# Gate work of part 1 in blocks of four pieces in every other step

## The chip, the cores and the metric

The kernel runs on one core of a Trainium2 chip. Times are device microseconds (us) of one execution. PE is TensorE (matmuls; PEld its weight loads), DVE VectorE, ACT ScalarE, POOL GpSimd, SP the engine that issues most DMAs. L12 is line 12 of the kernel.

## The reference

A gated recurrence over 4 batches of 8 heads, 768 positions and 48 values, and then a multiplicative feed-forward on its output, all float32:

```python
for t in range(S):
    state = alpha[:, :, t, :, None] * state + einsum('bhd,bhe->bhde', k[:, :, t], v[:, :, t])
    y[:, :, t] = einsum('bhd,bhde->bhe', q[:, :, t], state)
x = y.transpose(0, 2, 1, 3).reshape(3072, 384)
out = (((x @ w1) * (x @ w2)) @ w3) @ w_out      # w1, w2: 384 x 1024, w3: 1024 x 1024, w_out: 1024 x 384
```

## The kernel before

The recurrence is computed in 24 chunks of 128 positions, six to a batch. Part 1 is a loop over 25 steps (n = 0 to 24, L726); step n works on several chunks at once, as a pipeline. The feed-forward starts inside it: as soon as three or four chunks of x are there, the products x @ w1 and x @ w2 of these chunks (the "gates") are spread over the steps. The rest of the feed-forward follows after the loop (L824 on) on PE, with the weights w3 and w_out folded into one.

Float32 products that must be exact are made of three parts, high, low and mixed, each in a form that PE takes at its faster rate. So each factor of a gate is 3 x 3 = 9 matmuls (`products`, L554), and `exact` (L557) puts them together: parts 0 and 1 into one PSUM bank, copied by ACT (L563), part 2 into another, added by DVE (L565). [...]

**Pieces.** A piece is one factor of one gate: nine matmuls, one L563, one L565. Two pieces make a gate; the second one ends with the product of both factors on DVE (L602), and then the store of the gate before it is issued on SP (`store_ab`, L628). Gates wait in the queue `fill`, and `run(k)` (L691) takes k pieces from it. Four gates (eight pieces) come into it in steps 9, 13 and 17, eight gates (512 columns wide instead of 384) in step 21; before that `split_early` (L527; L521 on ACT, L522 and L524 on DVE) has split x.

**One step n from 10 on**, in the written order, with what it puts on the engines:

- loads for later steps on SP: alpha of n+5 (L145), k and q of n+4 (L151, L152), v of n+2 (L157), stores of x (L305);
- `attend_state(n-1)` (L474), which needs the state from `outer` and `advance`;
- `scores(n)` (L430), interleaved with `attend_low(n-1)` (L419); then the masks on DVE, four instructions of L440, which empty the two banks of the scores. `attend_low(n)` and `attend(n)` of the next step read the masked scores `ms`;
- `transposed(n+1)` (L381), copied to `qkT` by ACT (L383, two instructions); the scores of n+1 need it;
- in steps 9, 13, 17, 21 `split_early`;
- `attend(n-1)` (L482), copied by ACT (L489); `outer(n)` (L393, not in the last chunk of a batch: 5, 11, 17, 23), added by DVE (L403);
- the first piece, `run(pieces > 0)`;
- `decayed(n+2)` on DVE (L359) and `logs(n+4)` (L324, L328 on ACT, L329 on DVE);
- the second piece, `run(pieces > 1)`;
- `decays(n+3)` (L346), with two exponentials on ACT (L349, L350);
- one or two quarters of a weight conversion (`convert`: L245, L248, L251 to L253, L262, L265 on DVE; L244, L249, L260 on ACT);
- the third piece, `run(pieces > 2)`.

The order of each engine's queue is fixed before the kernel runs, by a planner that starts from the written order and may put an instruction ahead that it expects to be ready earlier. On PE the pieces stand in the trace where the code has them; on DVE, ACT and SP later work is often drawn forward. On the chip each engine works through its queue in that order.

The number of pieces in steps 10 to 24 is 3, 3, 2, 0, again and again: eight pieces in four steps.

Of the kernel before, what the change touches and what calls it, by code (L numbers as in the profile page):

```python
# [48 lines left out]
def kernel(  # L49
# [86 lines left out]
    def load_a(n):  # L136
        if paired(n):
            if n % 2 == 0:
                b, c = divmod(n, NCH)
                x = pairs[n // 2 % 2]  # L140
                nc.sync.dma_start(out=x.rearrange("p h s d -> p h (s d)"), in_=alpha[b, :, ds(c * C, 2 * C), :].rearrange("h (p s) d -> p h (s d)", s=2))
                st["a", n] = st["a", n + 1] = x
        elif n < N:
            st["a", n] = inp.tile([C, H, D], FP32, tag="ac", name="ac", bufs=2)
            nc.sync.dma_start(out=st["a", n], in_=rows(alpha, n))  # L145

    def load_kq(n):
        if n >= N:
            return
        st["kq", n] = inp.tile([C, 2, H, D], FP32, tag="kq", name="kq")  # L150
        nc.sync.dma_start(out=st["kq", n][:, 0], in_=rows(k, n))  # L151
        nc.sync.dma_start(out=st["kq", n][:, 1], in_=rows(q, n))  # L152

    def load_v(n):
        if n < N:
            st["v", n] = vs[n % len(vs)]
            (nc.gpsimd if 2 < n < 8 else nc.sync).dma_start(out=st["v", n][:, :, 0:D], in_=rows(v, n))  # L157
# [122 lines left out]
    def fetch(ahead=3):  # L280
        while weights and len(begun) < ahead:
            begun.append(weights.popleft())
            next(begun[-1])
# [17 lines left out]
    def store():  # L301

        while later:
            dst, src = later.popleft()
            nc.sync.dma_start(out=dst, in_=src)  # L305
# [109 lines left out]
    def attend_low(n, jj, i, half):  # L415

        s, w = ds(DP * i, DP), (vts[n % 2] if i else st["v", n])
        h = half * NP // 2 + jj
        nc.tensor.matmul(st["y", n][0][i][ds(DP * half, DP), jj, 0:DP], w[s, h if i else 2 * h, :],  # L419
                         st["ms", n][s, i, h, 0:DP], start=(n % NCH == 0 and jj == 0), stop=True, skip_group_check=True)  # L420
# [25 lines left out]
    def scores(n):  # L446
        if turned(n):
            return turned_scores(n)
        qkT = st["qkT", n]
        sc = [bank().rearrange("p (j c) -> p j c", j=NP) for _ in range(2)]  # L450
        for j in range(NP):
            for i in range(2):
                r = ds(DP * i, D)
                nc.tensor.matmul(sc[i][:, j, :], qkT[r, 0, j, :], qkT[r, 1, j, :], start=True, stop=True)  # L454
        ms = work.tile([C, 2, NP, C], FP32, tag="ms", name="ms")
        for i in range(2):
            masked = nc.vector.tensor_tensor(ms[:, i].bitcast(I32), sc[i].bitcast(I32), keep_bc, op=ALU.bitwise_and)
        ends_of_part1[0] = mark["ms", n] = masked.ins
        st["ms", n] = ms
# [3 lines left out]
    def attend_state(n):  # L463
        qkT = st.pop(("qkT", n))

        y = [bank()[:, 0:HP * C].rearrange("p (j c) -> p j c", c=C) for _ in range(2)]
        st["y", n] = y, [(half * HP + j, i, y[i][ds(DP * half, DP), j, :])
                         for j in range(HP) for i in range(2) for half in range(2)]  # L470
        if n % NCH:
            for j, i, to in st["y", n][1]:
                r = ds(DP * i, D)
                nc.tensor.matmul(to, Ts[n % 2][r, j, :], qkT[r, 1, j, :],  # L474
                                 start=(j % HP == 0), stop=False, skip_group_check=True)
# [25 lines left out]
    def load_early(e):  # L501

        first, chunks = EARLY[e]
        if chunks == 3:
            pieces = ((xb[0][:, XB - KM * TG:].bitcast(FP32), 3),)
        else:
            pieces = ((inp.tile([C, 2, H, D], FP32, tag="kq", name="kq").rearrange("p i h d -> p (i h d)"), 2),
                      *((inp.tile([C, H, D], FP32, tag="ac", name="ac", bufs=2).rearrange("p h d -> p (h d)"), 1) for _ in range(2)))
        st["xT", e], at = [], 0
        for x, width in pieces:  # L510
            x = x.rearrange("p (k t) -> p k t", k=KM)
            nc.sync.dma_start(out=x, in_=x_of(first + at, width))
            st["xT", e].append((x, ds(at * C, width * C)))
            at += width
# [176 lines left out]
    def run(pieces):  # L691

        for _ in range(pieces):
            if not fill:
                return
            try:
                next(fill[0])
            except StopIteration:
                fill.popleft()
# [22 lines left out]
    FIRST = 6  # L722
# [3 lines left out]
    for n in range(N + 1):  # L726
        if not 1 < n < FIRST:
            store()
        if n in loads:
            load_early(loads[n])  # L730
        if n != 1 and not 2 < n <= FIRST:
            load_a(n + 5)
        raws = (3, 3, 3, 3, 2, 2, 3, 3)[n] if n < 8 else 4
        for m in (n + 3,) * (n <= FIRST) + (n + 4,) * (n >= FIRST):
            load_kq(m)
            if 2 < n <= FIRST and m == n + 3:
                load_a(n + 5)
            if 1 < n < FIRST:
                store()
            if n < FIRST - 2:  # L740
                fetch(raws)
        if n >= FIRST:
            load_v(n + 2)
        if n:
            attend_state(n - 1)
        if n < N:
            scores(n)
        else:
            for j in range(NP):
                for i in range(2):  # L750
                    attend_low(n - 1, j % 2, i, i ^ (j < 2))
        transposed(n + 1)
        if n == 1:
            decays(3)
            load_a(6)
            with after_marks(("e", 3)):
                logs(4)
        if n == FIRST + 1:
            run(2)
        if n < FIRST:  # L760
            with after_marks("pool"):
                load_v(n + 2)
        if n - 2 in begin and n > FIRST:
            g, tiles = begin[n - 2]
            with after_marks(("ms", n), ("qkT", n + 1)):
                split_early(g)
            fill.extend(gate(g, f) for f in tiles)
        if n == FIRST:
            with after_marks("l", ("qkT", n + 1)):
                split_early(0)  # L770
            fill.extend(gate(0, f) for f in begin[n - 3][1])
        pieces = ((3, 3, 2, 0) if n > FIRST + 3 else (0, 3, 3, 0))[(n - FIRST) % 4] if n >= FIRST else 0
        if n == 0:
            with after_marks(("qkT", 0)):
                logs(2)
            decays(2)
            with after_marks(("e", 2)):
                logs(3)
        early, ready = n < FIRST, len(thirds) if n > 2 else n // 2
        marks = (*[("qkT", n + 1)] * (n < N - 1), *[("qk", n + 1), ("ms", n)] * early, *["x3"] * (n - 2 in begin and n > FIRST))  # L780
        if n < N - 2 and n != FIRST:
            with after_marks(*marks):
                convert(2 if early else 1, raws)
        advance(n)
        turn_v(n)
        if n:
            attend(n - 1)
        outer(n)
        if n > FIRST:
            third(ready)  # L790
        run(pieces > 0)
        if early:
            with after_marks(*marks):
                convert(1, raws)
        with after_marks(*[("ms", n)] * (n < 3)):
            decayed(n + 2)
        if not early:
            with after_marks(*[("qkT", n + 1)] * (n < N - 4)):
                logs(n + 4)
        if n == 4:  # L800
            load_early(0)
        convert(early and n > 0, raws)
        run(pieces > 1)
        if n:
            decays(n + 3)
        if n <= FIRST:
            third(ready)
        if 0 < n < FIRST:
            with after_marks(("e", n + 3)):
                logs(n + 4)  # L810
        if n == FIRST:
            with after_marks("x3", ("e", n + 3)):
                convert(2, raws)
        elif n < N - 2:
            convert(n == FIRST - 1 if early else n % 3 == 0, raws)
        if n == FIRST - 1:
            assert len(done) == 2 * KM
        run(pieces > 2)
        if n == N - 3:
            while begun:  # L820
                convert(1)
            weights.extend(load_out(j) for j in range(KF))
            fetch(4)
# [92 lines left out]
```

## Time and profile before

| | |
|---|---|
| median of 3 runs | 463.62 us (462.82 to 464.98) |
| profiled execution | 462.58 us, span 460.8 us |
| granted TensorE clock | 0.999 |
| PE, PEld busy | 444.3 us (96%), 393.4 us (85%) |
| DVE, ACT, POOL busy | 370.1 us (80%), 270.3 us (59%), 85.7 us (19%) |
| part 1 up to the first transpose of step 10 | 82.6 us |
| steps 10 to 21 | 82.6 to 168.2 us |
| steps 22 to 24 | 168.2 to 187.1 us |
| all after that | 187.1 to 460.8 us |

A step is read here from its first transpose (L381), which directly follows the scores, to that of the next step. So the stretch of step n holds the pieces of step n, and it ends with the scores of step n+1.

### The profile page before, as it was taken

Reading aid. Unit: us, or ns where it says so; the run is one execution under the profiler, and the core shown is the slowest. Engines: PE = TensorE matmul, PEld = TensorE weight load, DVE = VectorE, ACT = ScalarE, POOL = GpSimd, SP = SyncE. Lnnn points to the kernel's source line nnn. Section 1 sums busy time; section 2 is a strip of 40 time slices with the busy share of each in tenths; the row PEclk is TensorE's granted clock in tenths of the full one; section 3 lists DMA queues with packets and bytes.
Section 4 is the critical chain, followed back from the end, with each engine's and each line's share of the span. In section 5 each row is a group of like instructions: output and inputs, shape, how many; then the busy total and the mean of one; then the engine's idle time right before and its main releaser. Section 6 shows DMA issues by size and latency. Waiting matters only on the chain.

```text
span 460.8 us, 10652 instructions
## 1 busy us (share of the span) xinstructions
PE 444.3 (96%) x4080; PEld 393.4 (85%) x4080; DVE 370.1 (80%) x600; ACT 270.3 (59%) x507; POOL 85.7 (19%) x171
## 2 busy tenths in 40 slices
PE   4987999999999999999999999999999999999996
PEld 2665699898998988888888888888888999999996
DVE  2869997999989989798999899999537566776671
ACT  4775875758668653777975757566436333343430
POOL 6324232315314240012021010100000000000000
PEclk9999999999999999999999999999999999999999
DMA  9999999999998974445966364521119655665511
GB/s 177 259 206 218 266 221 201 243 214 212 188 233 181 242 179 156 155 112 161 301 198 211 116 172 133 177 68 46 48 51 282 203 151 167 187 186 162 155 53 51
DMA packets 149379, 79.95 MB, mean 173 GB/s; under 512 B 97184, under 2 KB 138784, under 8 KB 149328
## 3 DMA queue, kind: packets, MB, share of 16 engines
q1 hardware_dynamic: 143840, 64.84, 57.4%
q0 software_dynamic: 5488, 14.43, 10.5%
q8 instruction: 32, 0.52, 0.5%
q14 instruction: 19, 0.16, 0.1%
HBM read 57.19 MB, written 22.06 MB: 172 GB/s over the span
## 4 chain that ended last, share of the span: by engine, by line
PE 89%; DMA 4%; SPq 2%; DVE 2%; ACT 2%; issue 1%; DVEq 0%; ACTq 0%
PE bank L554 73%; PE bank L430 3%; PE bank L381 3%; PE bank L482 2%; PE bank L474 2%; DMA x<-in_alpha_dram 2%; PE bank L393 1%; DMA kq<-in_q_dram 1%; PE bank L346 1%; PE bank L419 1%; PE bank L343 1%; SPq L305 1%; SPq L145 1%; PE bank L454 1%; PE bank L485 1%
## 5 line engine op out<-in xcount | busy, mean ns | idle before, releaser
L554 PE MATMUL bank<-x,w 128*128 128x512 f32 (+1 forms) x688 | 163.0, 374 | 0.9 <-ACT qkT L383 0.9
L554 PEld LDWEIGHTS bank<-x,w 128*128 128x128 f32 x688 | 124.6, 188 | 21.1 <-ACT qkT L383 1.2
L554 PE MATMUL bank<-w3o,ab 128*128 128x384 f32 x576 | 100.2, 336 | 0.0
L554 PEld LDWEIGHTS bank<-w3o,ab 128*128 128x128 f32 x576 | 99.9, 188 | 0.2
L554 PE MATMUL bank<-x3b,w 128*128 128x512 f32 (+1 forms) x248 | 71.9, 385 | 0.0
L579 ACT ACTIVATE bank<-bank 128x512 f32<-128x512 f32 (+1 forms) x72 | 41.1, 573 | 34.2 <-PE bank L554 34.2
L554 PEld LDWEIGHTS bank<-x3b,w 128*128 128x128 f32 x248 | 46.4, 188 | 8.4
L628 POOL DMA_DIRECT2D abd<-r x33 | 19.3, 584 | 138.0 <-DVE r L614 116.2
L678 DVE TENSOR_TENSOR ab<-abl,ab 128x1024 fp32r<-128x1024 f32 x24 | 29.4, 1224 | 14.4 <-ACT ab L677 14.4
L383 ACT COPY qkT<-bank 128x512 f32<-128x512 f32 x48 | 26.2, 599 | 22.7 <-PE bank L381 22.7
L563 ACT ACTIVATE t<-bank 128x384 f32<-128x384 f32 x24 | 11.8, 493 | 45.9 <-PE bank L554 45.9
L677 ACT ACTIVATE ab<-abl 128x1024 fp32r<-128x1024 f32 x24 | 25.5, 1062 | 22.1 <-PE bank L554 19.8
L554 PE MATMUL bank<-wo,w3T 128*128 128x384 f32 x192 | 36.3, 337 | 0.0
L249 ACT ACTIVATE power<-power,rebias 128x512 uint32<-128x512 uint32 (+1 forms) x36 | 25.3, 702 | 17.2 <-DVE power L248 16.9
L554 PEld LDWEIGHTS bank<-wo,w3T 128*128 128x128 f32 x192 | 34.1, 188 | 1.2
L565 DVE SCALAR_TENSOR_TENSOR o<-bank,t 128x384 f32<-128x384 f32 x24 | 13.4, 558 | 25.9 <-issue 14.3
L359 DVE TENSOR_TENSOR qk<-kq,e 128x768 f32<-128x768 f32 x24 | 22.9, 954 | 13.8 <-ACT e L350 7.8
L614 DVE TENSOR_TENSOR r<-bank,r 128x512 f32<-128x512 f32 x32 | 21.8, 682 | 9.2 <-PE bank L554 7.7
L679 DVE SCALAR_TENSOR_TENSOR ab<-ab,abl 128x1024 fp32r<-128x1024 f32 x24 | 29.2, 1218 | 0.0
L565 DVE SCALAR_TENSOR_TENSOR r<-bank,r 128x384 f32<-128x384 f32 (+1 forms) x40 | 22.8, 576 | 7.4 <-ACT r L563 6.0
L563 ACT ACTIVATE r<-bank 128x384 f32<-128x384 f32 (+1 forms) x40 | 20.8, 526 | 13.1 <-PE bank L554 10.2
L251 DVE SCALAR_TENSOR_TENSOR mant<-mant,raw 128x512 f32<-128x512 uint32 (+1 forms) x36 | 23.4, 650 | 2.2 <-ACT raw L244 2.2
(115 smaller groups left out, 736.9 us busy)
## 6 DMA issues: line engine op xcount, KB each, us to landing
abl<-abd SPq DMA_DIRECT2D x24, 512.0 KB, 4.3
abd<-r POOLq DMA_DIRECT2D x33, 256.0 KB, 3.3
raw<-in_moe_w_dram SPq DMA_DIRECT2D x64, 128.0 KB, 4.0
raw<-in_moe_w_dram SPq DMA_DIRECT2D x12, 512.0 KB, 5.6
kq<-in_k_dram SPq DMA_DIRECT2D x24, 192.0 KB, 5.0
kq<-in_q_dram SPq DMA_DIRECT2D x24, 192.0 KB, 5.5
xd<-x SPq DMA_DIRECT2D x48, 96.0 KB, 4.0
xT<-xd POOLq DMA_DIRECT2D x6, 768.0 KB, 5.4
```

The source lines that it names most:

```text
L249: nc.scalar.activation(power, power, AF.Relu, scale=2.0 ** 23, bias=rebias)
L251: nc.vector.scalar_tensor_tensor(mant, top, 2.0 ** -20, rest, op0=ALU.mult, op1=ALU.add)
L359: mark["qk", n] = nc.vector.tensor_mul(qks[n % 3][:, :, :, 0:D], st.pop(("kq", n)), st.pop(("e", n)).rearrange("p i (h d) -> p i h d", h=H ...
L383: mark["qkT", n] = nc.scalar.copy(qkT[:, :, :, ds(DP * half, DP)], tp[half]).ins
L554: nc.tensor.matmul(p, w[part][i], x[part][i], start=start and part == parts[0] and i == 0, stop=stop and part == parts[-1] and i == n - 1, ...
L563: nc.scalar.activation(t, p1, AF.Copy, scale=(1.0 + 1.0 / P) * scale)
L565: nc.vector.scalar_tensor_tensor(to, p2, scale, t, op0=ALU.mult, op1=ALU.add)
L579: nc.scalar.activation(p, p, AF.Copy, scale=1.0 + 1.0 / P)
L614: nc.vector.tensor_mul(r[0], p, r[0])
L677: nc.scalar.activation(t[:, 0], ab, AF.Copy, scale=1.0 - 2.0 ** -13)
L678: nc.vector.tensor_sub(t[:, 1], ab, t[:, 0].bitcast(FP32))
L679: nc.vector.scalar_tensor_tensor(t[:, 2], t[:, 0].bitcast(FP32), -1.0 - 1.0 / P, ab, op0=ALU.mult, op1=ALU.add)
```

## The change

From step 10 on the pieces are 4, 0, 4, 0: the even steps have four, one at the first place, two at the second and one at the third; the odd steps have none. Four steps still have eight pieces. Step 13, 17 and 21 had none before either; steps 11, 15, 19 and 23 lose their three pieces, 10, 14, 18 and 22 get one more, 12, 16, 20 and 24 two more.

```diff
-        pieces = ((3, 3, 2, 0) if n > FIRST + 3 else (0, 3, 3, 0))[(n - FIRST) % 4] if n >= FIRST else 0
+        pieces = ((4, 0, 4, 0) if n > FIRST + 3 else (0, 3, 3, 0))[(n - FIRST) % 4] if n >= FIRST else 0
...
         convert(early and n > 0, raws)
-        run(pieces > 1)
+        run((pieces > 1) + (pieces > 3))
         if n:
             decays(n + 3)
```

## Prediction

> **What bounds the kernel now.** I read the page first (busy time, slices, chain), then the sums by stretch for steps 10 to 22, cut at each step's first transpose (L381), then the queues inside the steps without a piece.
>
> ```profile
> PE 444.3 (96%) x4080; PEld 393.4 (85%) x4080; DVE 370.1 (80%) x600; ACT 270.3 (59%) x507; POOL 85.7 (19%) x171
> PE   4987999999999999999999999999999999999996
> DVE  2869997999989989798999899999537566776671
> PE 89%; DMA 4%; SPq 2%; DVE 2%; ACT 2%; issue 1%; DVEq 0%; ACTq 0%
> ```
>
> PE carries the chain, but in the slices of part 1 DVE is as full as PE. The stretches of steps 10 to 13, 17, 21 and 22 to 24 (columns: time, then PE, PEld, DVE, ACT and POOL busy, clock, DMA):
>
> ```profile
> 82.61:92.59 9.98, 9.12 (x144) 8.24 (x141) 9.94 (x20) 7.24 (x18) 3.36 (x6) 1.00 0.96 224
> 92.59:100.93 8.34, 8.34 (x129) 7.71 (x127) 8.26 (x18) 4.69 (x11) 1.46 (x3) 1.00 1.00 222
> 100.93:107.62 6.69, 6.69 (x119) 6.25 (x116) 6.54 (x15) 5.17 (x12) 3.03 (x5) 1.00 0.97 184
> 107.62:111.87 4.25, 4.20 (x119) 3.54 (x116) 4.21 (x8) 3.69 (x9) 1.44 (x3) 1.00 0.98 191
> ...
> 136.68:140.36 3.68, 3.68 (x101) 3.06 (x98) 3.00 (x6) 2.93 (x6) 0.53 (x1) 1.00 1.06 214
> ...
> 164.75:168.17 3.42, 3.42 (x115) 3.23 (x113) 2.95 (x7) 2.67 (x6) 1.58 (x5) 1.00 0.63 180
> 168.17:187.05 18.88, 18.85 (x234) 15.07 (x231) 17.29 (x35) 7.88 (x18) 2.11 (x3) 1.00 0.47 144
> ```
>
> In steps 10 to 13 PE is busy 28.35 of 29.26 us and DVE 28.95: two engines at the limit, so little can be won. PE's one long wait is 0.9 us at 86.68, in the first piece of step 10, which stays where it is. The timelines of PEld and DVE in steps 13 and 15:
>
> ```profile
> 107.01 0.56 DVE L602 TENSOR_TENSOR r<-r 128x384 f32<-128x384 f32 x1
> 107.48 0.55 DVE L329 TENSOR_TENSOR la<-la,la 128x384 fp32r<-128x384 f32 x1
> 107.95 0.95 DVE L359 TENSOR_TENSOR qk<-kq,e 128x768 f32<-128x768 f32 x1
> 108.83 0.74 DVE L440 TENSOR_TENSOR ms<-bank,keep 64x256 int32<-64x256 int32 x2
> 109.60 0.87 DVE L440 TENSOR_TENSOR ms<-bank,keep_turned 64x256 int32<-64x256 int32 x2
> 110.58 0.24 PEld L430 LDWEIGHTS bank<-qkT 48*64 48x64 f32 x8 [0.27 <-ACT x L521]
> ...
> 121.11 0.95 DVE L359 TENSOR_TENSOR qk<-kq,e 128x768 f32<-128x768 f32 x1
> 121.98 0.55 DVE L565 SCALAR_TENSOR_TENSOR r<-bank,r 128x384 f32<-128x384 f32 x1
> 122.45 0.74 DVE L440 TENSOR_TENSOR ms<-bank,keep 64x256 int32<-64x256 int32 x2
> ```
>
> Here is the loop that limits a step without pieces: scores on PE, masks (L440) on DVE, next scores. In step 13 the scores end at 107.62, the masks start at 108.83 (a lag of 1.21, DVE finishing L602, L329 and L359), end at 110.47, and the next L430 loads at 110.58. The trace names ACT's L521, but the masks end as closely before it. In step 15 the lag is 1.64 and nobody notices: three pieces of PE work follow.
>
> **The change part by part.** *PE work:* none added or removed. Steps 10 to 21 keep 24 pieces (216 matmuls of L554; nine take 1.57 in the chain), steps 22 to 24 keep 8. Pieces move from steps 11, 15, 19 and 23 into their neighbours.
>
> *New steps without pieces.* Between scores and next scores PE then has L381 0.65, L482 0.62, L393 0.45, L346 0.35 to 0.55 and L474 0.60: 2.77 us, or 2.32 in steps that end a batch (11, 17), where L393 is missing. DVE needs lag + 1.64 (four masks) + 0.14 to the load. PE's wait is lag + 1.78 - 2.77 (or 2.32). On the old steps it gives 0.22 for step 13 (0.27 in the row), 0.10 for step 17 (lag 0.64) and none for step 21 (lag 0.18). So the price hangs on the lag.
>
> - Upper end: today's lags stay, 2.09 in step 11, 1.64 in 15, 2.19 in 19 (first L440 against first L381: 94.68 and 92.59, 122.45 and 120.81, 150.90 and 148.71). Waits: 1.55 + 0.65 + 1.20 = 3.4 us.
> - Lower end: lags like today's empty steps, mean 0.7: 0.2 us, from step 11 alone.
> - Middle: after the decays (L346) of a four-piece step PE still has one piece 1.57, L474 0.60 and scores 0.87, 3.04 us. In it DVE must do L329 0.55, L359 0.95, two L565 1.10 and L602 0.56, 3.16 us, starting about 0.6 late, after ACT's copy of la (L328, 0.52): a lag near 0.7. In steps 11 and 19 the planner has also put a part of a weight conversion there (L262 and L265, 1.36; L251 to L253, 2.0). With half of that I take a lag of 1.4: 0.86 + 0.41 + 0.41 = 1.7 us.
>
> *Step 23 to 24.* Scores of step 23 end at 178.45; masks run from 179.62 to 181.26; 6.49 us of pieces hide them. Without these PE has L482 0.62 and L474 0.60 before L419 needs the masks: 1.17 + 1.78 - 1.22 = 1.7 us at most, nothing if the planner puts pieces of step 24 first. I take a third, 0.6, since the rows show PE in the written order.
>
> *Steps that were empty before* (13, 17, 21) follow a fuller step; the last piece still ends just before them, and L329 comes a piece earlier relative to it. Their waits (0.3 together) and slow first pieces (step 14 took 8.94 where step 15 took 8.77) may shrink: 0 to 0.9, I take a gain of 0.4.
>
> *Moved with the pieces.* Per gate one store of r (SP), two L563 on ACT, two L565 and one L602 on DVE. Behind a store on SP's queue stand the loads of alpha, k, q and v; they have reserve. The tightest today are v of step 14, landed at 112.16 for an L393 at 113.03, and v of step 18, 140.39 for 141.52, both after an empty step. Those of 12, 16 and 20 have 5.6, 5.5 and 8.0 us and lose 4.7 less 1.57, 3.1. If that cover went, a landing takes about 4 us. Alpha's L324 held ACT 2.1 us at 116.79 and cost PE under 0.2; in step 16 its reserve of 2.4 becomes a wait of 0.7: nothing. POOL's decay chain keeps one long step in each pair: nothing. After the loop PE runs unbroken for 270 us with the same work: nothing.
>
> *Sum:* +1.7 + 0.6 - 0.4 = +1.9 us. The profiled execution took 462.58 (span 460.8 and 1.8 around it): 464.5. The median of the runs, 463.62, lies 1.04 above it: **465.5**.
>
> **The rivals.** Within 0.5% is 2.3 us either way, about what a measurement of this kernel can tell from no change.
>
> *The masks come fully late* (slower). The planner orders DVE as in the rows above, with conversions ahead of the masks, and PE pays each lag whole: 3.4 + 1.7 = 5.1 us, 468.7; with the usual gain 468.3. It decides from a mean lag of about 2 us. For it: DVE has 0.3 us idle in steps 10 to 13, so late work cannot catch up. Against it: DVE idles 2.2 in step 16 and 1.8 in step 20, and each wait of PE lets DVE catch up.
>
> *A bank wait as in step 10* (slower). At 86.68 a piece waited 0.9 for L383, which stood on ACT behind L249, which waited for DVE. Such a wait after each new empty step (12, 16, 20) costs 2.7 in place of the 1.7: 466.5. Against it: DVE's three-us split, which caused it, falls in none of these steps.
>
> *Everything stays hidden.* Lags below 1, pieces of step 24 ahead of the masks, and the old waits gone: +0.2 - 0.9, 462.9. For it: four pieces give DVE up to ten us in which conversions can go ahead, and this is the lag of the old empty steps.
>
> *Longer runs of weight loads* (faster). PEld is busy 92.69 of 104.44 us over these stretches. If a run of pieces closed the 0.63 that PEld idles in a three-piece step (8.34 less 7.71), in all twelve steps, that is 7.6 us: 456.0. Against it: that idle time lies at the small matmuls, whose number stays. [...]
>
> **How the numbers follow.** The forecast (+0.5 to +3.2) has 0.56, the masks fully late 0.18, the bank wait 0.06, all hidden 0.17, longer runs 0.03. Of the forecast about a quarter, 0.14, lies above +2.3. Slower: 0.14 + 0.18 + 0.06 = 0.38. Faster: 0.03. The rest, 0.59, is no difference that can be told. The range runs from all hidden, 462.9, to the masks fully late, 468.7; it leaves out longer runs and part of the scatter of the runs (462.82 to 464.98). The forecast's own range is 464.1 to 466.8.
>
> **What would show it.** In the profile after: stretches of steps 11, 15 and 19 of about 3.6 to 5 us, with L430 loading 0.14 after the last L440; a gap before L419 of step 24; steps 10, 12, 14 near 10 us; the clock at 1.00; the rest after the loop 270 us. Wrong if L430 starts well after the masks and PE still waits (a landing or a bank), if the planner moved pieces into the empty steps, or if the 270 us change.

## The result, and the profile after

| | kernel before | changed kernel |
|---|---|---|
| median of 16 runs each | 462.59 us (461.06 to 464.98) | 465.72 us (464.6 to 470.75) |
| ratio | | 1.0079 (95% interval 1.006 to 1.0097) |
| profiled execution | 462.58 us, span 460.8 us, clock 0.999 | 465.32 us, span 463.6 us, clock 0.999 |

The changed kernel is slower by about 0.8%, 2.8 to 4.5 us. Ratios, here and below, are taken over the fast runs and are not the quotients of the medians, which would be 1.0068 here. The time lies 0.2 us from the forecast of 465.5 us and inside its range. But the forecast called it most likely no difference that can be told, and the time is one that can be told. The new page, in the lines that answer to those shown of before:

```profile
PE 444.3 (96%) x4080; PEld 394.0 (85%) x4080; DVE 370.9 (80%) x600; ACT 271.4 (59%) x507; POOL 85.7 (18%) x171
PE   4898999998999999999999999999999999999996
DVE  2869997999888889999998899999436667776671
PE 81%; DVE 7%; DMA 3%; ACT 3%; SPq 2%; issue 2%; POOL 0%; DVEq 0%; ACTq 0%; POOLq 0%
```

Busy times are the same to about a microsecond, so no work was added. The chain has PE at 81% instead of 89% and DVE at 7% instead of 2%: the chain now passes over DVE in places where it stayed on PE. The sums by stretch (steps 10 to 13, 19, and 22 to 24):

```profile
81.25:92.85 11.60, 10.71 (x153) 9.80 (x150) 11.55 (x23) 7.84 (x19) 3.42 (x6) 1.00 0.87 205
92.85:97.67 4.82, 4.16 (x101) 3.25 (x99) 4.78 (x12) 3.22 (x8) 1.33 (x3) 1.00 0.93 207
97.67:107.51 9.84, 9.84 (x136) 9.40 (x135) 9.21 (x19) 6.23 (x14) 2.04 (x4) 1.00 1.09 210
107.51:113.09 5.58, 4.29 (x118) 3.61 (x115) 5.07 (x10) 4.79 (x10) 2.97 (x5) 1.00 1.12 253
...
151.39:156.71 5.32, 4.39 (x118) 3.70 (x115) 5.28 (x12) 3.73 (x9) 3.56 (x7) 1.00 1.06 247
...
170.42:189.30 18.88, 18.45 (x231) 14.93 (x229) 17.89 (x38) 10.35 (x24) 2.11 (x3) 1.00 0.49 150
```

Steps 11, 13 and 19 are the ones of these where PE (second column) newly stands: 0.66, 1.29 and 0.93 us; the 0.89 us of step 10 were there before (0.86). In steps 11 and 19 DVE (fourth column) is busy for all but 0.04 us. Steps 10 to 21 take 89.17 us against 85.56 (+3.61), and the rest from step 22 on 293.18 against 292.63 (+0.55). The part before step 10, which the change does not touch, was 1.36 shorter in this execution: 3.61 + 0.55 - 1.36 = 2.8, the difference of the spans.

Step 11 on DVE and PE, after its first transpose at 92.85:

```profile
93.06 0.55 DVE L602 TENSOR_TENSOR r<-r 128x384 f32<-128x384 f32 x1
93.53 0.95 DVE L359 TENSOR_TENSOR qk<-kq,e 128x768 f32<-128x768 f32 x1
...
94.39 0.42 DVE L245 TENSOR_SCALAR mant<-raw 128x512 uint32<-128x512 uint32 x1
...
94.73 0.74 DVE L440 TENSOR_TENSOR ms<-bank,keep 64x256 int32<-64x256 int32 x2
95.50 0.86 DVE L440 TENSOR_TENSOR ms<-bank,keep_turned 64x256 int32<-64x256 int32 x2
...
95.62 0.55 PE L474 MATMUL bank<-qkT,T 48*64 48x128 f32 x10 [0.52 <-DVE ms L440]
...
96.42 0.23 PEld L430 LDWEIGHTS bank<-qkT 48*64 48x64 f32 x8 [0.39 <-DVE ms L440]
...
154.66 0.67 PE L474 MATMUL bank<-qkT,T 48*64 48x128 f32 x16 [0.93 <-DVE ms L440]
```

The masks come 1.88 us after the first transpose, behind work left from step 10 (L602, L359) and a conversion part (L245). The loop of scores, masks and next scores that the prediction describes is there. It stops PE at two places: L430 as foreseen, and already L474, which needs a bank that the masks empty (all of part 1 takes its banks from one pool, L93). Step 19 looks the same (lag 2.38; L474 waits 0.93, the last row). Step 13 has another wait, on POOL:

```profile
109.93 0.20 POOL L410 TENSOR_TENSOR dec<-dec 128x4 f32<-128x4 f32 x1 [4.52 <-PE bank L346]
110.19 1.80 POOL L165 COPY vt<-v 64x192 f32<-64x192 f32 x2
...
112.05 0.27 PE L419 MATMUL bank<-ms,vt 64*64 64x64 f32 x1 [1.29 <-POOL vt L165]
```

The turned copy of v (L165) stands behind L410 of the next chunk's decay. v itself had landed at 104.67. The row names L346 as what ended L410's wait, but that is a coincidence: L410 reads what a load (`dec<-ends`, L367) brings, issued on POOL at 104.72 and landed at 109.76, and in the profiles of before, after, changed_again and less_dve_before alike L410 starts 0.17 us after this landing.

### The profile page after: what moved, and what is told of

It reads as the page before. It is cut to its first block, busy times and chain, and to the rows that moved or that the text cites. A ratio compares the mean times of both kernels' runs of the same rounds, so it can differ in the third digit from the quotient of the medians.

```text
span 463.6 us, 10657 instructions
## 1 busy us (share of the span) xinstructions
PE 444.3 (96%) x4080; PEld 394.0 (85%) x4080; DVE 370.9 (80%) x600; ACT 271.4 (59%) x507; POOL 85.7 (18%) x171
## 4 chain that ended last, share of the span: by engine, by line
PE 81%; DVE 7%; DMA 3%; ACT 3%; SPq 2%; issue 2%; POOL 0%; DVEq 0%; ACTq 0%; POOLq 0%
PE bank L554 69%; PE bank L381 2%; PE bank L430 2%; DVE qk L359 1%; DMA kq<-in_q_dram 1%; PE bank L482 1%; PE bank L343 1%; PE bank L393 1%; PE bank L474 1%; DVE ms L440 1%; DVE r L565 1%; PE bank L346 1%; PE bank L419 1%; DMA xd<-x 1%; DMA ac<-in_alpha_dram 1%
## 5 line engine op out<-in xcount | busy, mean ns | idle before, releaser
L678 DVE TENSOR_TENSOR ab<-abl,ab 128x1024 fp32r<-128x1024 f32 x24 | 29.4, 1225 | 15.2 <-ACT ab L677 15.2
L383 ACT COPY qkT<-bank 128x512 f32<-128x512 f32 x48 | 26.1, 598 | 24.5 <-PE bank L381 24.5
L563 ACT ACTIVATE t<-bank 128x384 f32<-128x384 f32 x24 | 11.8, 493 | 45.7 <-PE bank L554 45.7
L359 DVE TENSOR_TENSOR qk<-kq,e 128x768 f32<-128x768 f32 x24 | 22.9, 956 | 14.3 <-ACT e L350 9.2
L565 DVE SCALAR_TENSOR_TENSOR o<-bank,t 128x384 f32<-128x384 f32 x24 | 13.4, 558 | 25.0 <-issue 14.3
L563 ACT ACTIVATE r<-bank 128x384 f32<-128x384 f32 (+1 forms) x40 | 20.9, 525 | 15.0 <-PE bank L554 15.0
L679 DVE SCALAR_TENSOR_TENSOR ab<-ab,abl 128x1024 fp32r<-128x1024 f32 x24 | 29.2, 1218 | 0.0
L565 DVE SCALAR_TENSOR_TENSOR r<-bank,r 128x384 f32<-128x384 f32 (+1 forms) x40 | 22.9, 578 | 4.7 <-ACT r L563 3.1
```

The lines of the kernel that those rows point to most:

```text
L359: mark["qk", n] = nc.vector.tensor_mul(qks[n % 3][:, :, :, 0:D], st.pop(("kq", n)), st.pop(("e", n)).rearrange("p i (h d) -> p i h d", h=H ...
L383: mark["qkT", n] = nc.scalar.copy(qkT[:, :, :, ds(DP * half, DP)], tp[half]).ins
L563: nc.scalar.activation(t, p1, AF.Copy, scale=(1.0 + 1.0 / P) * scale)
L565: nc.vector.scalar_tensor_tensor(to, p2, scale, t, op0=ALU.mult, op1=ALU.add)
L678: nc.vector.tensor_sub(t[:, 1], ab, t[:, 0].bitcast(FP32))
L679: nc.vector.scalar_tensor_tensor(t[:, 2], t[:, 0].bitcast(FP32), -1.0 - 1.0 / P, ab, op0=ALU.mult, op1=ALU.add)
```

## The experiments

All times are medians; the kernel before is the one timed in the same session.

**Which waits repeat.** The changed kernel once more, unedited.

> The changed kernel itself, run again, to see which of its waits repeat. Theory: the waits that come from the plan repeat (lag of the masks in steps 11 and 19, 1.2 to 1.3 us of PE each; about 0.5 before L554 in step 18; 0.6 before L419 in step 24), the 1.3 us at L419 in step 13 (vt of L165) does not or is replaced by a wait of about 0.6 in step 14; steps 10 to 21 take 88 to 89.3 us against 85.6, and the median is 2.5 to 3.7 us above the kernel before. Rival, the waits are scatter of the one profiled execution: another set of waits, and a sum of steps 10 to 21 below 87.5.

Measured: 465.5 us (before 463.85), ratio 1.0058 (1.0033 to 1.0083). Steps 10 to 21 took 87.91 us in its profile. Steps 11 and 19 wait as before (4.66 and 5.28 us long), and so does L419 in step 24. Step 13 took 4.06 us without the POOL wait; step 14, 10.22 in the first profile, took 10.90. L165 stands behind L410 here too, and the load of `dec` landed at about the same time, 109.67; but step 13 began 1.0 us later, at 108.51, and so did not wait for it. So the POOL wait is scatter of one execution, with a smaller loss in step 14 in its place, and the late masks are the plan's. The sum by pairs of steps in this profile, which has no accident of its own, is the best account of the change. First before, then this run; pairs 10-11, 12-13, 14-15 and 18-19; columns as above:

```profile
82.61:100.93 18.32, 17.46 (x270) 15.95 (x268) 18.20 (x37) 11.93 (x29) 4.82 (x9) 1.00 0.98 223
100.93:111.87 10.94, 10.89 (x234) 9.79 (x232) 10.75 (x22) 8.86 (x20) 4.46 (x8) 1.00 0.97 187
111.87:129.59 17.72, 17.72 (x287) 16.39 (x284) 16.95 (x33) 11.36 (x28) 6.62 (x13) 1.00 1.04 219
...
140.37:157.67 17.30, 17.26 (x271) 15.89 (x268) 17.18 (x33) 12.27 (x29) 8.07 (x15) 1.00 0.91 190
```

```profile
82.67:98.74 16.07, 14.72 (x251) 13.03 (x248) 15.98 (x34) 10.98 (x27) 3.08 (x7) 1.00 0.95 212
98.74:112.57 13.83, 13.83 (x250) 12.95 (x249) 12.55 (x25) 9.54 (x21) 4.37 (x9) 1.00 1.11 223
112.57:127.43 14.86, 14.68 (x266) 13.41 (x264) 14.46 (x28) 9.77 (x24) 6.70 (x13) 1.00 1.04 226
...
141.24:156.94 15.70, 14.46 (x251) 13.01 (x248) 15.61 (x30) 11.24 (x27) 8.35 (x15) 1.00 0.94 200
```

The change moves two pieces, about 3.1 us of PE, from the first pair of each four steps to the second. The second pairs grow by what PE got: 2.89, and 3.03 and 3.14 in the pairs 16-17 (10.78 to 13.81) and 20-21 (10.50 to 13.64). The first pairs shrink by 2.25, 2.86 and 1.60 only, since DVE does not lose as much: two pieces are two L565 and one L602, 1.66 us. (DVE's busy time in these pairs fell by 2.22, 2.49 and 1.57, so other work of its queue changed places too.) In the pairs 10-11 and 18-19, where DVE was full before (18.20 of 18.32, 17.18 of 17.30), DVE is full again and PE is not. In the pair 14-15 PE was the full engine, DVE had 0.77 us left, and the move is nearly free. In all +0.64, +0.17 and +1.54 us for the three groups.

**Order of the queues.** Two kernels change only the order in which POOL, or DVE, gets the changed kernel's work.

```diff
# pool_order: the decay product waits for the turned v
+        with after_marks(*[("vt", n - 1)] * turned(n - 1)):
             nc.gpsimd.tensor_mul(dec, d[:, 0, :], d[:, 1, :])
...
# masks_first: in odd steps from 11 on, L359 and conversions of that step behind the masks
+        marks = (..., *[("ms", n)] * (n > FIRST + 3 and n % 2 == 1 and n < N))
...
-        with after_marks(*[("ms", n)] * (n < 3)):
+        with after_marks(*[("ms", n)] * (n < 3 or n > FIRST + 3 and n % 2 == 1 and n < N)):
             decayed(n + 2)
```

> The changed kernel with one order kept on POOL: the decay product of step 14 (L410) may not stand ahead of the turned copy of v of step 13 (L165); all other queues are as in the changed kernel. Theory (POOL's queue): in the changed kernel L410 waits 4.5 us for its DMA with v already there, the copy comes at 110.19 and PE waits 1.5 us at L419. That wait goes, step 13 takes about 4.2 us instead of 5.58, and the time falls by 1.3 to 1.5 us against the changed kernel (about 1.0045 of before). Rival (DVE's sum binds): DVE's split for step 14 is the next late thing, the wait turns up at the first piece of step 14, and the time stays.

Measured: 467.39 us (before 462.85), ratio 1.0092 (1.0064 to 1.0119). L419's wait in step 13 is gone (step 13 took 4.06 us), but step 14 took 10.92 and nothing was won. As changed_again shows the same without the edit, the edit decided nothing. The median is 1.7 us above that of the changed kernel, not below it: five of the six runs had a mean granted clock below 0.998, and in the profile the clock was at half from 45.38 to 52.20, before any step that the change touches, and from 158.02 to 161.43.

> The changed kernel with another order on DVE: in odd steps from 11 on the conversions of that step and its product q, k with e (L359) may not stand ahead of the masks (L440). PE, ACT and POOL have the same order. Theory (lag of the masks): the lag in steps 11 and 19 falls from 1.9 and 2.4 us to about 0.6, PE's waits of 1.3 and 1.2 us there become 0.1 and 0, and the time falls by about 2.4 us against the changed kernel (about 1.003 of before). Rival (DVE's sum binds): the work put back stalls the next step, at L381 waiting for L359 or at the pieces, and less than half of it is won.

Measured: 467.47 us (before 462.85), ratio 1.0119 (1.0087 to 1.015). The masks' lag in step 11 fell to 0.05 us, in step 19 only to 1.52: two conversion parts left from step 18 (L252 and L253, which start at 152.41 and 153.49) still stand ahead of the masks there. Steps 10 to 21 took 87.34 us, only 0.57 less than in changed_again. The median says less than this: four of the six runs had a clock below 0.998, and the profile has half the clock from 53.20 to 56.61, before step 10. The waits of PE from step 10 to step 24 (columns: us, times, longest; without the old one of step 10):

```profile
PE bank L554 <- DVE ms L440: 0.7, 2, 0.4
PE bank L554 <- DVE x L522: 0.6, 1, 0.6
PE bank L381 <- DVE qk L359: 0.5, 1, 0.5
PE bank L474 <- DVE ms L440: 0.5, 1, 0.5
```

The work that had stood ahead of the masks is now late itself: L359 holds the next transposes (L381), and the split (L522) and the masks hold later pieces. Steps 10 to 13, where the masks did come first, took 28.91 us instead of 29.90 in changed_again, but steps 14 to 17 took 29.36 instead of 28.67, and steps 18 to 21 29.07 instead of 29.34. So the late masks of step 11 are worth about 1 us, and most of it came back in the next four steps. An order that favours the masks mostly moves the wait to another row of DVE.

**Less work on DVE.** Low and mixed parts (L262, L265) of five weight tiles are replaced by zeros from POOL, 6.8 us less on DVE by the instructions' durations, once in the changed kernel and once in the kernel before. By the pages DVE's busy time fell by 5.1 and 4.7 us.

```diff
-        mark["l"] = nc.vector.scalar_tensor_tensor(l, h.bitcast(FP32), -P, w, ...
+        if len(done) <= 2 * KM:
+            mark["l"] = nc.vector.scalar_tensor_tensor(l, h.bitcast(FP32), -P, w, ...
         done.append((i, kk, half))
+        if len(done) > 2 * KM + 1:
+            with after_marks("pool"):
+                for x in (l, m):
+                    nc.gpsimd.memset(x.bitcast(FP32), 0.0)
-        if half:
+        elif half:
```

> The changed kernel with less work on DVE: of five weight tiles converted in steps 10 to 21 the low and mixed parts (L262, L265, 1.36 us a tile, 6.8 us in all) are set to zero by POOL instead; these two parts are left out of the result. Theory (DVE is behind in the empty steps): of the 3.1 to 3.6 us that steps 10 to 21 take longer than before (88.1 in the run with 3, 3, 2 at the end and 89.2 in the changed kernel, against 85.6) at least 2 go; the masks of steps 11 and 19 start less than 1 us after the scores. Rival (the waits come of the order and of the banks, not of DVE's sum): steps 10 to 21 stay over 87.5 us.

> The same 6.8 us of DVE work taken from the kernel before; the same two parts are left out. Theory: steps 10 to 21 have only about 2.5 us of PE waits there, 1.0 of them in step 10 behind the split: they fall from 85.6 by 1 us at most, and the difference to the changed kernel with less DVE work shrinks to under 1.5 us. Rival (blocks of four cost the same whatever DVE does): the difference stays at 2.5 us or more.

Measured: 466.77 us with the change (463.51 to 471.1) and 462.66 without it (461.71 to 464.8), beside 463.54 for the kernel before: ratios 1.0062 (1.0031 to 1.0093) and 0.9983 (0.9963 to 1.0004). By the medians blocks of four cost as much with less work on DVE, as the rival says. But that does not settle it. In six of the ten runs of less_dve_changed the mean clock was below 0.998, and in its profile the L563 of step 18 waited 1.81 us for the store of r, a second mechanism that is shown below. Its four other runs have a median of 463.72, and the nine of less_dve_before at a clock of 0.998 or more one of 462.58: by these few runs the difference is 1.1 us, under the theory's 1.5.

The profiles don't decide it either. In that of less_dve_changed steps 10 to 21 took 87.21 us, 0.7 less than in changed_again and 2.0 less than in the first profile of the change: under the rival's 87.5 and at the edge of the theory's 2 us. In step 11 other conversion parts (L245, L248) fill the room ahead of the masks; in step 19 the masks stand behind L565 and L602, which the late L563 holds. Steps 11 and 19 took 4.73 and 5.49 us with lags of 1.69 and 2.02, where less than 1 was expected, and L474 still waited 1.4 us in three places for the masks.

The profile of less_dve_before missed its expectation of 85.6 or less by far: steps 10 to 21 took 89.12 us. It was that kernel's longest run (464.8). An L563 of step 12 waited 1.74 us in it for the store of r, the masks of step 13 came 2.35 us late and L474 waited 0.91; so that wait is not a matter of blocks of four alone.

What can be said is that DVE's total alone does not set the wait; what stands ahead of the masks at that moment counts as well. Together with masks_first: changing the order alone, or the amount alone, moves or leaves most of the late masks' price. Both at once were not tried.

**Where the price lies.** The pattern 4, 0, 4, 0 in some of the steps only, 3, 3, 2, 0 in the others:

```diff
-        pieces = ((4, 0, 4, 0) if n > FIRST + 3 else (0, 3, 3, 0))[...]
+        pieces = ((4, 0, 4, 0) if 13 < n < 18 else (3, 3, 2, 0) if n > FIRST + 3 else (0, 3, 3, 0))[...]
# last_3_3_2: FIRST + 3 < n < N - 2;  blocks_10_13: 9 < n < 14;  blocks_18_21: 17 < n < 22
```

> The change in steps 10 to 21 only; steps 22 to 24 have 3, 3, 2 pieces again. Theory: PE's wait of 0.6 us at L419 of step 24 for the masks of step 23 goes and nothing else moves: 0.6 us less than the changed kernel. Rival: the end of part 1 plays no part, since the phase after it absorbs the wait: no difference.

Measured: 465.0 us (before 462.85), ratio 1.0053 (1.0028 to 1.0079). L419's wait in step 24 is gone. The interval is too wide for 0.6 us, but the profile's row says where it was.

> Blocks of four in steps 14 to 17 alone (4, 0, 4, 0), all else 3, 3, 2, 0 as before. Theory: the price lies in the eight steps around 10 to 13 and 18 to 21, where DVE has conversions in front of the masks; steps 14 to 17 took 28.56 us in the run with 3, 3, 2 at the end and 28.50 before. So the time is that of before within 0.5 us (0.999 to 1.001). Rival (each empty step costs): half of a third of the loss, 1 us or more.

Measured: 463.61 us (before 463.54), ratio 1.0002 (0.9983 to 1.0021): no price in the middle group, as expected. In its profile steps 14 to 17 took 29.15 us against 28.50; but steps 10 to 13 and 18 to 21, which it leaves as before, took 29.62 and 28.38 against 29.26 and 27.81, so a single execution scatters by as much.

> 4, 0, 4, 0 in steps 10 to 13 alone, 3, 3, 2, 0 after them. Theory, prices of the groups add up: 1.1 to 1.3 us (the late masks of step 11, with steps 12 and 13 even), so 463.5 to 464.7 for a kernel before of 462.4 to 463.5. Rival, the work that DVE leaves behind is carried on and is paid in later groups: 0.5 or less here. Other rival, later groups lose because this one was changed: 2 us or more here.

Measured: 463.71 us (before 463.85), ratio 1.0005 (0.9988 to 1.0022). In its profile steps 10 to 13 took 30.44 us against 29.26, the 1.2 that was expected, with L474 waiting 0.6 in step 11. The runs do not show it; the interval allows at most 1.0 us. The size of this group's price stays between 0 and 1.

> 4, 0, 4, 0 in steps 18 to 21 alone. Theory, prices of the groups add up: 1.2 to 1.5 us (L554 in step 18 and the late masks of step 19), so 463.6 to 465.0. Rival, the lag of step 19 comes from work that DVE carries over from the groups before: 0.5 us or less here.

Measured: 468.2 us (before 463.85), ratio 1.0096 (1.0072 to 1.012), more than the whole change. No theory had this. The timeline of ACT and PE in its step 19, and then the sums of the stretch from 155.19 to 162.01, with the granted clock in the last column but two:

```profile
152.31 0.49 ACT L563 ACTIVATE r<-bank 128x384 f32<-128x384 f32 x1 [3.59 <-DMA abd<-r]
...
152.85 0.67 PE L393 MATMUL bank<-v,qk 128*64 128x48 f32 x16 [1.41 <-ACT r L563]
...
156.13 1.13 PE L474 MATMUL bank<-qkT,T 48*64 48x128 f32 x16 [2.07 <-DVE ms L440]
```

```profile
155.19:162.01 6.82, 5.88 (x112) 5.68 (x112) 6.27 (x14) 3.12 (x8) 2.65 (x6) 0.50 1.01 253
```

The L563 of step 18's fourth piece waits 3.59 us for the store of an older r, issued on SP at 148.31 behind a load of v and landed at 152.22. L563 holds ACT's copy of the next transposes, so PE stands 1.41 us, then the masks are late and it stands 2.07 more, to 156.13. From 155.19, within that second wait, its clock is at half for 6.82 us. The fourth piece in a row needs the buffer that the store issued after the second piece sets free. In the changed kernel the same row came just in time: store issued at 146.05, landed 149.25, L563 at 149.89.

**The buffer of r.** blocks_18_21 with a fifth buffer for r from step 18 on, every queue in the same order.

```diff
+    gx, count = pool("gx", 1, stack=part1, side="right"), [0]
-            r.append(gw.tile([C, width], FP32, tag="g", name="r"))
+            r.append((gx if 23 < count[0] < 48 and count[0] % 5 == 4 else gw).tile([C, width], FP32, tag="g", name="r"))
+            count[0] += 1
```

> Blocks of four in steps 18 to 21 alone, as in blocks_18_21, with a fifth buffer for r in these steps; every engine's queue has the same order. Theory: the 3.5 us that PE stood in step 19 of blocks_18_21 began with the fourth piece of step 18, whose L563 waited 3.59 us for the store of an older r (issued at 148.31, landed 152.22), and the half clock of 6.8 us after it followed from PE's standing. With the fifth buffer the L563 does not wait, steps 18 to 21 take 28.5 to 30 us (33.6 in blocks_18_21, 28.1 before), the clock is 0.998 or more in most runs, and the time is 463.5 to 465. Rival, the standing comes from the late masks and DVE's queue, which reach L474 anyway, and the L563 is a bystander: steps 18 to 21 stay above 31 us, the clock stays at 0.991 to 0.996, 467 or more.

Measured: 464.03 us (before 463.11), ratio 1.0026 (1.0006 to 1.0046). The wait of L563 and the half clock are gone from the profile; steps 18 to 21 took 29.13 us (33.80 without the fifth buffer). What is left of PE's waiting in steps 18 and 19 is the masks:

```profile
PE bank L474 <- DVE ms L440: 1.1, 1, 1.1
```

So most of what blocks_18_21 cost, 0.7% by the two ratios and 4.5 us by the two spans, was one missing buffer, and 29.13 - 27.81 = 1.3 us are the price of blocks of four in this group. Of the 4.5 us the waits account for 2.4 (1.41 + 2.07 against 1.1); the half clock is the likely rest.

The profiles of the kernels that differ in the pattern alone (before, the change twice, last_3_3_2 and the three blocks_ kernels without the buffer) say the same: steps 10 to 13 took 29.3 to 29.6 us with 3, 3, 2, 0 and 29.9 to 31.8 with blocks of four; steps 14 to 17 28.4 to 28.9 and 27.9 to 29.2; steps 18 to 21 27.8 to 28.4 and 29.2 to 29.4, or 33.8 with the wait for the buffer.

**All at once.** The edits of pool_order, masks_first and last_3_3_2 together.

> The three edits together (POOL's order, the masks first in odd steps, 3, 3, 2 pieces at the end) on the 4, 0, 4, 0 pattern. If the three waits are the whole cost, the time is that of the kernel before, or up to 0.8 us less, because its small waits in steps 13, 14 and 19 are gone: 0.998 to 1.001 of before. If blocks of four cost something else, by the bank waits or DVE's sum, 2 us or more stay: 1.004 or more.

Measured: 466.32 us (before 462.85), ratio 1.0074 (1.004 to 1.0108). Steps 10 to 21 took 87.43 us, as with masks_first alone. The edits do not add up to a repair, which fits a wait that only changes its place. As with masks_first, four runs (of seven) had a clock below 0.998, and the profile has half the clock from 52.72 to 56.13, before step 10.

**The old wait of step 10.** In the kernel before, L383 stands behind a conversion in step 10 and holds a piece 0.9 us. The edit moves the conversion quarters of step 9 to steps 10 and 11.

```diff
-                convert(2 if early else 1, raws)
+                convert(2 if early or n in (10, 11) else n != 9, raws)
...
-            convert(n == FIRST - 1 if early else n % 3 == 0, raws)
+            convert(n == FIRST - 1 if early else n % 3 == 0 and n > 9, raws)
```

> The kernel before, with the two conversion quarters of step 9 moved to steps 10 and 11, so that on ACT L383 (copy of qkT for step 11) stands ahead of L249. Theory: the 0.9 us that a piece of step 10 waits at 86.68 for the bank that L383 empties come from L249, which waits for DVE behind the split. The wait goes and the time falls by 0.8 to 1.0 us against before (0.998). Rival: the piece waits for the split (L522, L524) anyway, which ends at 84.7, or the conversion delays the masks of step 10: no gain.

Measured: 462.36 us (before 463.54), ratio 0.9977 (0.9957 to 0.9998). Step 10 took 9.28 us instead of 9.98; all of steps 10 to 21 took 85.20 instead of 85.56, since step 15 became 0.47 longer. This is the one version with the whole result that is faster than both kernels, by 0.2% with an interval that just excludes no difference.

## Why the prediction was right or wrong, step by step

**The loop without pieces: right mechanism, right rule, wrong lags.** The prediction's wait of lag + 1.78 - 2.77 (or 2.32) gives 1.34 us in step 11 and 1.39 in step 19 with the lags of the profile after, 1.88 and 2.38. Against steps 17 and 15, which have the same content and no wait (3.51 and 3.97 us), steps 11 and 19 were 1.31 and 1.35 us longer; changed_again gives 1.14 and 1.32 in the same way. The wrong term is the lag of 1.4 taken for all three steps. After the change it was 1.88 and 2.38 in steps 11 and 19, near the old 2.09 and 2.19, and 0.13 in step 15. So the term of +1.7 (0.86 + 0.41 + 0.41) measured 2.7 in the profile (1.31 + 1.35, nothing in 15) and 2.5 in changed_again. The prediction had both facts that tell them apart: conversion parts ahead of the masks in 11 and 19 and not in 15. It then averaged them. Taking the upper end for the two and the lower for the third would have given 1.55 + 1.20 = 2.75.

**Step 24: +0.6, right.** From step 22 on it took 0.55 and 0.59 us longer in the two profiles; L419 waits 0.4 for the masks by the waits of PE. With 3, 3, 2 in these steps again (last_3_3_2) that part took 292.9 us, against 293.2 with the change and 292.6 before. The reason given, PE in the written order, holds.

**The old empty steps: -0.4, not borne out.** Steps 13 and 17 did get shorter, from 4.25 to 4.06 and from 3.68 to 3.52 us in changed_again. But steps 14 and 18, after an old empty step, then lost time: step 14 took 10.90 us where step 16 with the same four pieces took 10.29. In step 18 a piece waits 0.34 us for the masks' bank, and in last_3_3_2 the first piece of step 14 waits 0.41 for it; in step 14 of changed_again 0.44 of the 0.61 us lie ahead of the first piece, at L482, where the profile names nothing that was waited for. With +2.35 in all of steps 10 to 21 and 2.46 in steps 11 and 19, this term is -0.1. The prediction's second rival, a bank wait in a long step after an empty one, thus came in small part, but after steps 13 and 17 and not after the new empty ones, and from the masks on DVE and not from L383.

**"Nothing" for what moves with the pieces: right as it fell out, but for a thin reason.** It spoke of loads behind the stores on SP. It left out who waits for the stores: the fourth piece's L563, which needs the buffer. In the profile after, that had 0.64 us to spare; in blocks_18_21 it had none and ACT waited 3.59 us. POOL's chain, put at nothing, held PE 1.3 us in step 13 of one of two profiles, and step 14 was 0.7 shorter there.

**The sum.** +1.9 was predicted; by the profiles changed_again has 2.5 - 0.1 + 0.6 = 2.9, from 462.58 to 465.5 us. That the forecast fell on the time to 0.2 us is luck: it stood on a median of three runs, 463.62, and sixteen runs gave 462.59. An error of one microsecond in the base hid one of the same size in the sum. The change itself is not known to a microsecond: the medians differ by 3.13 us in the first session and by 1.65 in that of changed_again, where the kernel before took 463.85.

**The rivals.** *Masks fully late* was right for steps 11 and 19 and wrong for 15 and 24. *Everything hidden* was right for the middle group. *Longer runs of weight loads* did not come: step 12, with four pieces and no wait, has PEld idle for 0.44 us and takes 9.84 us, and the pair 12-13 grew by 2.89 us in changed_again, about what two pieces cost.

**What the sum leaves.** The changed kernel's runs reach to 470.75 us, and those above 468 were runs with a mean clock below 0.998. Of its 27 runs in two sessions 11 were such, of the 88 runs of the kernel before in the four later sessions 19. So part of the ratio of 1.0079 is probably time at half clock: in the session of changed_again the runs at 0.998 or more have medians of 465.36 us (six runs) and 463.62 (sixteen of the kernel before), 1.7 us apart. That it follows PE's waits is supported by blocks_18_21 alone, where all six runs were below 0.998, and three of twelve with the fifth buffer; for the changed kernel it is argued. In pool_order, masks_first and all_three the profile has the half clock before step 10 too, so not all of it comes from the waits that are told of here.

## What to carry to other kernels

Work taken out of a step of an in-order pipeline shortens it only until the next full engine (in changed_again about 3.1 us of PE work left the pair 10-11, which became 2.25 us shorter, with DVE busy for 15.98 of its 16.07 us): compare each engine's busy time with the length of the steps that lose work, not of those that gain it, and read for each step which rows stand ahead of the one that is waited for. Average no lags over steps whose queues differ. When more of the same work comes in a row, count its buffers too, to the landing of the store that frees each (the L563 of blocks_18_21 waited 3.59 us for one).

## What the runs showed of the hardware

TensorE's granted clock fell to half inside a running kernel: for 6.82 us in blocks_18_21, in the second of two waits of PE of 3.5 us together, and in pool_order, after a wait of 1.5 us at L474, for one stretch of half that length:

```profile
158.02:161.43 3.41, 3.41 (x66) 3.17 (x59) 3.38 (x7) 1.34 (x4) 0.93 (x2) 0.50 0.92 230
```

The other stretches at half clock that are told of here had the same two lengths: 6.82 us in pool_order (45.38 to 52.20), 3.41 in masks_first (53.20 to 56.61) and in all_three (52.72 to 56.13). PE did not stand for the whole of the 3.41 us before such a fall: in blocks_18_21 it stood 2.2 us of those before 155.19 in two parts (151.78 to 152.85 and 154.06 to 155.19) and worked between them; in pool_order it stood 1.54 us of those before 158.02. Nor does PE's standing time alone decide: in masks_first PE stood 0.71 us from 49.79 to 53.20, and the clock fell; in the first profile of the change it stood 2.19 us without a break, up to the L276 at 36.20, and the clock was full from 33.50 to 40.32. What decides it is open. In blocks_18_21 the waits of 3.5 us were followed by more loss than their own length (the span is 4.5 us longer than with the fifth buffer, where PE still waits 1.1), so the clock column is to be read together with the waits.

The rates of the two forms of float32 products show in the profile of before: on the chain, two plain ones of 128x384 (L340, at 17.77) took 1.50 us, two of that size in the form of the parts (L346, at 97.38) 0.35 us.
